# A list scheduler for hand tables in an attention and feed-forward kernel, with softmax normalised per head after the weighing

## Chip, cores and metric

The kernel runs on one core of one Trainium2 chip. The metric is device time in microseconds (us) for one launch. The engines are PE (TensorE, matrix products; PEld is its weight load), DVE (VectorE), ACT (ScalarE), POOL (GpSimd) and SP (SyncE, which issues all DMAs here). Each works through its own queue in order.

## The reference

Two batches, eight heads, 768 positions, 64 features a head. Queries and keys are hashed to 64 buckets by the signs of six projections. The scores of pairs in unequal buckets are masked, a softmax follows, and the result is weighed with v:

```python
mask = q_bucket[:, :, :, None] == k_bucket[:, :, None, :]
scores = np.where(mask, scale * np.matmul(q, k.transpose(0, 1, 3, 2)), -1000000000.0)
attn = np.exp(scores - np.max(scores, axis=-1, keepdims=True))
attn = attn / (np.sum(attn, axis=-1, keepdims=True) + 1e-09)
x = np.matmul(attn, v)        # then (1536 tokens, 512)
h = x @ w_in                  # 512 x 2048
x = (h * (1.0 / (1.0 + np.exp(-h)))) @ w_out
out = ((x @ w1) * (x @ w2) @ w3) @ w_out2   # 512 x 1024, 1024 x 1024, 1024 x 512
```

q, k, v and the projections are float32; the weights are float64.

## The kernel before

Every product is made of three float32r products: an operand is split into a rounded part (h) and the float32r of the rest (l), and h·h, h·l and l·h add up in PSUM. So splitting (a rounding copy, then a subtraction) runs all through the kernel.

**Weights.** A weight comes in pieces of 1024 columns and two steps of 512 columns each (`Piece`, `Step`, lines 125 to 191). A step is one DMA of 512 KB with the float64 words, two scaling copies on ACT (`scale`: the high words as a float, L165, and the low words, L169), two joins on DVE (`join`, L178 and L182; the second puts the sign bit back), and the split on POOL (`split`: L114 rounds, L117 subtracts). Seven pieces and four raw buffers exist.

**Attention.** w3 @ w_out is made ahead, as `wprime`, beside the attention (`combine`, L442: 8 blocks of 24 products), so that the second feed-forward part needs one product less. Two heads form a `Pair` (q and k transposed, a head on each half of the partitions): loads, rounding, rest, projection (L266), bucket bits (L273), then DMAs that gather the operands of each head's scores (L298, L304). A `Unit` is 128 queries of one head, 96 in all:

- `scores` (L342): four products of 384 columns, the mask being part of the operands.
- `peak`, `factor`, `offset` on DVE (L349, L354, L360): the row's negated maximum, 0.125 or 0, and their product. The last has two tensors of one column as inputs.
- `exp` on ACT (L365), with scale and bias from these columns; the instruction also leaves the row's sum.
- `guard` and `invert` on DVE (L372, L376): sum plus 1e-9, and its reciprocal. `norm` on POOL (L379) multiplies the 768 columns of P with it.
- `turn` on PE (L388): six transposes. `split`: ACT rounds (L120, tile `pth`), DVE subtracts (L406, `ptl`).
- `weigh` on PE (L417), for two units at a time: 12 products of 256 columns. `store`: two copies on ACT (L120, `xt` and `X`), one addition on POOL (L431) into X, the tokens' features.

**Order.** It is written by hand. A loop over slots (lines 550 to 590) emits for each slot the steps of up to six units in different stages, then what the tables give for it: `PAIRS` (lines 45 to 55) has the slots of the pairs' jobs, `STEPS` (57 to 79) those of the weights, `FILL` (81 to 86) the number of w3 products, `ON_DVE` what DVE does in POOL's place.

**Feed-forward.** 1536 tokens are three blocks of 512. `Ff1` has 24 cells (8 pieces by 3 blocks) of 48 products, `Ff2` 12 cells of 72: 2016 products of 512 columns. A cell rises (`up_mm`, L194 to L196, then sigmoid on ACT, L655, or a copy, L689, the gate on DVE, L657 or L694, and `split_g`, L602 and L603) and falls (L194 to L196 again, added to X on DVE, L672 or L709). The loop of lines 722 to 729 lets the next cell rise before the last one falls. The steps of the weights still to come are spread over it by `tick` and `advance` (lines 609 to 629). The first rise of a block takes x split by `split_x` (L222, L223). The outputs leave by DMA at L711.

PSUM has eight banks: during the attention four for scores (two tensors of two banks), two for transposes, one for the weighed output, one for w3 products and projections; in the feed-forward eight, four for rises and four for falls.

## Time and profile before

| | |
|---|---|
| median of 3 runs | 782.79 us (782.45 to 785.75) |
| span of the profiled execution | 781.3 us, 11396 instructions |
| busy share: PE, PEld, DVE, ACT, POOL | 96%, 82%, 71%, 55%, 45% |
| queue of SP's DMAs | 26384 packets, 74.14 MB |

The profile is of one execution; its own time is not given apart from its span, from the first to the last instruction. Times of the trace are counted from the span's start. Busy times of PE contain the overlap of pipelined products, so the distance between starts is what a product costs in a row. An idle time in a row is what the engine stood still before it, with the instruction that ended it.

### The profile page before, as it was taken

To read this page: it belongs to the slowest core of one execution; us is meant where nothing else is said; L and a number is where in the kernel's file an instruction comes from. 1 tells how busy PE (TensorE), PEld (TensorE's weight loads), DVE (VectorE), ACT (ScalarE), POOL (GpSimd) and SP (SyncE) were. 2 spreads that over 40 slices of the span, in tenths; PEclk is the share of its full clock that TensorE was granted. 3 is DMA by queue.
4 is the path that set the end of the run, shared out by engine and by line. 5 is a ranking of instruction groups with operands and counts; after the bars stand their busy time and mean duration, and the time that the engine had idled before them with its cause. 6 is when DMAs were issued, how large, how long until landed. Compare 5 with 4: busy or idle time off the path is not lost.

```text
span 781.3 us, 11396 instructions
## 1 busy us (share of the span) xinstructions
PE 746.4 (96%) x3858; PEld 636.9 (82%) x3858; DVE 556.8 (71%) x1153; ACT 429.9 (55%) x848; POOL 348.2 (45%) x364
## 2 busy tenths in 40 slices
PE   6888999899999999999999999999999999999997
PEld 5777888789898888788888888888888888888885
DVE  5999999999999898966777776666685224444233
ACT  4787979799898889775444433432334432221110
POOL 3889888687878677423333322204150102102000
PEclk8689999999999999999999999999999999999999
DMA  8867464646383431322232312203020002000012
GB/s 272 214 178 172 128 154 130 152 143 162 85 207 75 116 122 40 123 81 92 98 101 88 107 58 78 65 16 108 17 90 29 28 27 80 29 0 1 1 54 109
DMA packets 26442, 74.86 MB, mean 96 GB/s; under 512 B 4136, under 2 KB 4136, under 8 KB 26384
## 3 DMA queue, kind: packets, MB, share of 16 engines
q1 hardware_dynamic: 26384, 74.14, 32.8%
q8 instruction: 31, 0.51, 0.3%
q14 instruction: 27, 0.22, 0.1%
HBM read 49.29 MB, written 5.24 MB: 70 GB/s over the span
## 4 chain that ended last, share of the span: by engine, by line
PE 58%; DVE 1%; issue 0%
PE dps L194 6%; PE dps L196 6%; PE dps L195 6%; PE hps L195 5%; PE hps L196 5%; PE hps L194 5%; PE ops L196 3%; PE pb L196 3%; PE pa L196 3%; PE ops L195 3%; PE pb L195 3%; PE pa L195 3%; PE pb L194 3%; PE pa L194 3%; PE ops L194 3%; DVE x L223 1%
## 5 line engine op out<-in xcount | busy, mean ns | idle before, releaser
L379 POOL TENSOR_SCALAR P<-P,st 128x768 f32<-128x768 f32 x96 | 96.5, 1005 | 54.2 <-DVE st L360 46.5
L120 ACT ACTIVATE gh<-g 128x512 fp32r<-128x512 f32 x72 | 45.6, 633 | 114.8 <-DVE g L694 66.2
L365 ACT ACTIVATE P<-sc,st 128x768 f32<-128x768 f32 x96 | 95.0, 989 | 12.7 <-DVE st L360 9.9
L406 DVE TENSOR_TENSOR ptl<-pt,pth 128x384 fp32r<-128x384 f32 x192 | 97.3, 547 | 5.4 <-ACT pth L120 5.1
L603 DVE TENSOR_TENSOR gl<-g,gh 128x512 fp32r<-128x512 f32 x72 | 62.3, 866 | 50.3 <-ACT gh L120 50.3
L349 DVE TENSOR_REDUCE st<-sc 128x1 f32<-128x768 f32 x96 | 91.1, 948 | 9.8 <-PE sc L342 8.0
L120 ACT ACTIVATE pth<-pt 128x384 fp32r<-128x384 f32 x192 | 83.6, 487 | 22.5 <-PE pt L388 21.7
L388 PE MATMUL pt<-ident,P 128*128 128x128 f32 x576 | 82.7, 281 | 11.8 <-POOL P L379 8.0
L114 POOL TENSOR_SCALAR w<-x_w 128x512 fp32r<-128x512 f32 x32 | 20.3, 633 | 158.0 <-DVE x_w L182 137.5
L388 PEld LDWEIGHTS pt<-ident,P 128*128 128x128 f32 x576 | 68.0, 145 | 23.4 <-POOL P L379 17.3
L417 PE MATMUL xo<-pth,V 128*128 128x256 f32 x288 | 81.7, 311 | 4.5 <-ACT X L120 4.2
L694 DVE TENSOR_TENSOR g<-pb,a 128x512 f32<-128x512 f32 x24 | 16.6, 690 | 92.0 <-PE pb L196 92.0
L417 PE MATMUL xo<-ptl,V 128*128 128x256 f32 x288 | 75.5, 290 | 3.5 <-DVE ptl L406 3.4
L195 PE MATMUL dps<-gl,wo 128*128 128x512 f32 x192 | 74.7, 389 | 0.0
L194 PE MATMUL dps<-gh,wo 128*128 128x512 f32 x192 | 74.7, 389 | 0.0
L196 PE MATMUL dps<-gh,wo 128*128 128x512 f32 x192 | 74.7, 389 | 0.0
L655 ACT ACTIVATE sg<-hps 128x512 f32<-128x512 f32 x48 | 28.3, 590 | 80.9 <-PE hps L196 80.9
L417 PEld LDWEIGHTS xo<-pth,V 128*128 128x128 f32 x288 | 55.9, 194 | 11.7 <-ACT X L120 8.9
L417 PEld LDWEIGHTS xo<-ptl,V 128*128 128x128 f32 x288 | 56.3, 195 | 5.3 <-DVE ptl L406 5.0
L442 PE MATMUL wps<-wo,w 128*128 128x512 f32 x192 | 59.0, 409 | 0.0
L342 PE MATMUL sc<-ka,qa 128*128 128x384 f32 x192 | 52.7, 357 | 5.6 <-DMA ka<-khi 3.4
L657 DVE TENSOR_TENSOR g<-hps,sg 128x512 f32<-128x512 f32 x48 | 33.0, 687 | 35.1 <-ACT sg L655 35.1
(187 smaller groups left out, 1913.7 us busy)
## 6 DMA issues: line engine op xcount, KB each, us to landing
raw_w<-in_w SPq DMA_DIRECT2D x32, 512.0 KB
raw_wo<-in_wo SPq DMA_DIRECT2D x24, 512.0 KB
raw_win<-in_win SPq DMA_DIRECT2D x16, 512.0 KB
ka<-khi SPq DMA_DIRECT2D x31, 192.0 KB
qraw<-in_qT SPq DMA_DIRECT2D x8, 384.0 KB
kraw<-in_kT SPq DMA_DIRECT2D x8, 384.0 KB
qa<-qhi SPq DMA_DIRECT2D x16, 192.0 KB
qb<-qhi SPq DMA_DIRECT2D x16, 192.0 KB
```

Source lines behind the costliest of these rows:

```text
L120: nc.scalar.activation(out=dst, in_=src, func=AF.Copy)
L194: nc.tensor.matmul(out=ps, lhsT=whi, rhs=xhi, start=first, stop=False)
L195: nc.tensor.matmul(out=ps, lhsT=whi, rhs=xlo, start=False, stop=False)
L196: nc.tensor.matmul(out=ps, lhsT=wlo, rhs=xhi, start=False, stop=last)
L349: nc.vector.tensor_reduce(out=s[:, 0:1], in_=self.sc[:, :, :HF], op=ALU.max, axis=AX.XY, negate=True)
L365: nc.scalar.activation(out=self.P, in_=self.sc[:, :, :HF], func=AF.Exp, scale=s[:, 1:2], bias=s[:, 2:3], accum_out=s[:, 3:4],)
L379: nc.gpsimd.tensor_scalar(out=self.P, in0=self.P, scalar1=self.st[:, 4:5], scalar2=1.0, op0=ALU.mult, op1=ALU.mult)
L388: nc.tensor.transpose(pt[:, c * 128:c * 128 + 128], self.P[:, g, c * 128:c * 128 + 128], ident)
L406: nc.vector.tensor_tensor(out=l, in0=src, in1=h.bitcast(F32), op=ALU.subtract)
L417: nc.tensor.matmul(out=self.xo[:, :N], lhsT=V[:, c, :], rhs=x[:, c, :], start=(c == 0 and x is self.h), stop=(c == NQ - 1 and x is self.l),)
L442: nc.tensor.matmul(out=ps, lhsT=w[:, a, k], rhs=r[:, b], start=(k == 0 and n == 0), stop=(k == 7 and n == 2))
L603: nc.vector.tensor_tensor(out=l, in0=g, in1=h.bitcast(F32), op=ALU.subtract)
```

## The change

The tables and the slot loop go. Each step of the work becomes an `op` with its engines and their costs in ns, the steps that it depends on, a due time, the buffers that it takes and gives back, and a function that emits it. `Plan.run` then goes through a modelled time: of the engines' ready steps it takes, for each engine, the one that is due first among those that could start within 150 ns of the earliest, and emits the engine's that starts soonest. Steps with more than one engine in their `on` go where the plan puts them. `OFF` moves the due times of each kind of step by a fixed number of us. The due times assume 3 us a unit. w3 products have a `hold` as well, before which the plan does not emit them. In the feed-forward the same plan orders the rises, falls, gates and weight steps of all cells.

Of the computation:

- q is scaled by 0.125 first (`prescale`), and `factor` is then two operations of one tensor each.
- P is not normalised. The row sums of a head gather in `sums`; once a head, DVE adds 1e-9 and inverts (`invert`), PE transposes the inverses (`flip`), ACT unloads them, a DMA stores them to DRAM, a second spreads them over 64 partitions, and POOL multiplies the head's 768 columns of x (`norm`).
- Groups of three units are weighed at once (12 products of 384 columns); the two copies behind go to ACT or DVE (`move`).
- Steps of weights due in the attention get their sign from an activation (`side`) and a product on POOL (`signed`) in place of the second join; scaling the low words may go to POOL; for pieces needed in the first 120 us the split may go to ACT and DVE.
- Feed-forward part one uses tanh of h/2: (tanh + 1) times h, halved as it is added (`more_`).
- Scores, qa, qb, ka and kb have two buffers (the latter had three), raw weights three and one more later (four before). Each PSUM tensor is allocated once for its bank or pair of banks.
- At the hand-over (`hand_over`) the attention's memory is given back and six more PSUM banks join the two for products.

The core of the diff, with the scheduler's choice, the weights, a unit and a head:

```diff
-PAIRS = [
-    dict(zip(JOBS, row))
...
-STEPS = {
...
-FILL = [
...
+SOON, W3_AT, W3_SPAN = 120, 34.7, 23.6
+OFF = {
+    "exp": 1.57, "factor": -0.43, "fall": -3.11, "gate": 5.08, "hi": -5.82, "high": -4.16, "join": -2.5,
+    "lo": -5.04, "low": -1.83, "more_": 8.78, "move": 1.81, "norm": -3.78, "peak": 6.41, "prescale": 1.59,
+    "project": -1.13, "rest": -7.4, "rise": -14.66, "round_": -1.66, "scores": -2.64, "side": -5.88,
+    "sign": 5.02, "signed": -1.18, "split_lo": 5.08, "squash": 6.92, "store": -8.8, "turn": 0.04, "vhi": 3.17,
+    "vlo": -9.35, "weigh": 4.85, "weight": -1.47,
+}
...
+        while todo:
...
+            for e, t in engines.items():
+                could = []
+                for o in wait[e]:
+                    s = max(t, o.ready)
+                    if e == "POOL" or (e == "DVE" and o.port):
+                        s = max(s, port)
+                    for pool, key in o.take:
+                        slots = self.free[pool]
+                        if not slots or (pool in turn and turn[pool][-1] != key):
+                            s = None
+                            break
+                        s = max(s, min(slots, key=lambda x: x[0])[0])
+                    if s is None:
+                        continue
+                    could.append((s, o))
+                if could:
+                    soon = min(s for s, _ in could) + self.PATIENCE
+                    at, pick = min((x for x in could if x[0] <= soon), key=lambda x: (x[1].due, x[0]))
+                    if best is None or at < best[0]:
+                        best = at, e, pick
...
-        def join(self, n, cut=slice(0, STEP)):
...
+                def side(e, raw=raw, x=x):
+                    nc.scalar.activation(out=plan[x], in_=pair(raw)[:, :, 1].bitcast(F32), func=AF.Sign)
+
+                def signed(e, x=x, t=t):
+                    nc.gpsimd.tensor_tensor(out=plan[x], in0=plan[t].bitcast(F32), in1=plan[x], op=ALU.mult)
+                a = op({"ACT": 570}, high, [load], due, [("x", x)])
+                b = op({"ACT": 570, "POOL": 590}, low, [load], due, [("t", t)])
+                j = op({"DVE": 608}, join, [a, b], due + 1, port=True)
+                if need < T_END - 20:
+                    j = op({"ACT": 570}, side, [j], due + 2, give=[raw])
+                    j = op({"POOL": pool2(STEP)}, signed, [j], due + 2.5, give=[t])
+                else:
+                    j = op({"DVE": 608}, sign, [j], due + 2, give=[raw, t], port=True)
...
+            soon = need < BEGIN + SOON
+            h = op({"POOL": pool1(STEP), "ACT": act(STEP)} if soon else {"POOL": pool1(STEP)}, hi, [j, opener], due + 3, take=first)
+            opener = h
+            done.append(op({"POOL": pool2(STEP), "DVE": dve(STEP)} if soon else {"POOL": pool2(STEP)}, lo, [h], due + 4,
...
-            def factor(self):
...
-            def norm(self):
...
+                def factor(e, uk=uk):
+
+                    s = plan[uk("st")]
+                    nc.vector.tensor_scalar(
+                        out=s[:, 1:2], in0=s[:, 0:1], scalar1=BIG / 2, scalar2=1.0, op0=ALU.is_lt, op1=ALU.mult
+                    )
+                    nc.vector.tensor_scalar(
+                        out=s[:, 2:3], in0=s[:, 0:1], scalar1=BIG / 2, scalar2=s[:, 0:1], op0=ALU.is_lt, op1=ALU.mult
+                    )
...
+                sc = op({"PE": 4 * (PE_FREE + HF * PE_COL)}, scores, gathers[par], tu - 3, [("S", uk("S"))])
+                pk = op({"DVE": dve(S)}, peak, [sc], tu - 2.8, [("st", uk("st"))])
+                fa = op({"DVE": 195}, factor, [pk], tu - 2.8)
+                ex = op({"ACT": 985}, exp, [fa, *exps[:1]], tu - 2.7,
+                        [("P", uk("P"))] + ([("sums", hk("sums"))] if i == 0 else []), [uk("S"), uk("st")])
...
+                    tr = op({"PE": 3 * PE_TURN}, turn, [ex, begun, tr if g else None], tu + 0.5, [("T", uk(f"T{g}"))],
+                            give=[uk("P")] if g else [])
+                    opens = g == 0 and i % GRP == 0
+                    a = op({"ACT": act(HF)}, split_hi, [tr, None if opens else opener], tu + 1,
+                           [("pth", gk("pth")), ("ptl", gk("ptl"))] if opens else [])
+                    opener = a if opens else opener
+                    low.append(op({"DVE": dve(HF)}, split_lo, [a], tu + 1.5, give=[uk(f"T{g}")]))
...
+                mv = op({"ACT": 2 * act(N), "DVE": 2 * dve(N)}, move, [xo], tu + 3.5, [("xt", gk("xt"))], [gk("xo")])
+                stores.append(op({"POOL": pool2(N)}, store, [mv], tu + 4, give=[gk("xt")]))
...
+            iv = op({"DVE": 250}, invert, exps, te + 3)
+            fl = op({"PE": 110}, flip, [iv], te + 4, [("W", hk("it"))], [hk("sums")])
+            un = op({"ACT": act(128)}, unload, [fl], te + 4.5, [("wsb", hk("invt"))], [hk("it")])
+            sp = op({"SP": 350}, dma(lambda h=h: inverse[h].rearrange("(i p) -> i p", p=128), lambda hk=hk: plan[hk("invt")][:NQ, :128]),
+                    [un], te + 8, give=[hk("invt")], size=3072)
+            bc = op({"SP": 500}, dma(lambda hk=hk, m=m: plan[hk("invb")][m], lambda h=h: inverse[h:h + 1].to_broadcast([64, S])),
+                    [sp], te + 12, [("invb", hk("invb"))], size=196608)
+            nm = op({"POOL": pool2(S)}, norm, [bc, *stores], te + 20, give=[hk("invb")])
+            last_store[h] = nm
...
+            last = op({"PE": 3 * (PE_FREE + 512 * PE_COL)}, product, [last, *made, *(x for p in wo2p for x in p[1])],
+                      need + k * span / 8 - 2, [("fill", key + ("token",)), ("W", key + ("ps",))] if k == 0 else [],
+                      ([name] + [p[0] for p in wo2p] * (it == DF2 // 128 - 1)) if k == 7 else [],
+                      hold=need + k * span / 8 - 2)
...
+    def hand_over(e):
+        st.close()
+        mp = pool("mp")
+        for bk in (1, 2):
+            xs[bk] = [tiles(mp, f"x{s}{bk}", [128, BLK], F32R, 4) for s in "hl"]
+        plan.buffers("sg", tiles(mp, "sg", [128, BLK], F32, 4))
+        plan.buffers("gh", tiles(mp, "gh", [128, BLK], F32R, 6))
+        plan.buffers("gl", tiles(mp, "gl", [128, BLK], F32R, 6))
+        plan.buffers("raw", tiles(mp, "rawm", [128, 2 * STEP], U32, 1))
+        plan.buffers("fill", [None] * 7)
+        plan.buffers("W", tiles(pool("mps", PSUM), "more", [128, 512], F32, 6))
...
+                def gate(e, key=key, sg=sg):
+                    nc.vector.scalar_tensor_tensor(
+                        out=plan[sg], in0=plan[sg], scalar=1.0, in1=plan[key], op0=ALU.add, op1=ALU.mult
+                    )
+
+                a = op({"ACT": act(BLK)}, squash, [last], d, [("sg", sg)])
+                g = op({"DVE": dve(BLK)}, gate, [a], d + 0.7, give=[key, key + ("token",)])
```

## Rows read from the trace of the kernel before

**Rows 1.** Busy us by stretch: PE, PEld, DVE, ACT, POOL; granted clock, DMA share, GB/s

```profile
0.00:316.00 316.00, 287.59 (x1840) 258.77 (x1841) 291.67 (x775) 264.47 (x565) 238.48 (x254) 0.96 0.55 145
20.00:60.00 40.00, 33.90 (x179) 30.14 (x177) 36.60 (x91) 33.15 (x67) 33.66 (x32) 0.76 0.73 189
60.00:160.00 100.00, 90.47 (x604) 81.19 (x605) 98.51 (x256) 83.97 (x182) 79.87 (x83) 1.00 0.60 154
160.00:316.00 156.00, 150.88 (x1015) 137.18 (x1014) 145.24 (x409) 138.09 (x301) 118.56 (x128) 1.00 0.42 113
326.00:776.00 450.00, 449.95 (x1984) 371.94 (x1983) 254.56 (x368) 158.10 (x271) 102.78 (x105) 1.00 0.17 58
```

**Rows 2.** Instructions in order of time: a gather, the first scores, the feed-forward's first products

```profile
6.31 0.69 SPq L298 DMA_DIRECT2D ka<-khi  x1
...
12.42 0.98 PE L342 MATMUL sc<-ka,qa 128*128 128x384 f32 x2 [3.45 <-DMA ka<-khi]
...
316.42 0.40 PE L194 MATMUL hps<-qhi,win 128*128 128x512 f32 x1
...
319.05 0.50 PE L195 MATMUL hps<-vraw,win 128*128 128x512 f32 x1 [0.73 <-DVE vraw L223]
```

**Rows 3.** The exponential's line by stretch (ACT busy, records, granted clock, DMA share, GB/s)

```profile
20.00:60.00 40.00, 11.45 (x21) 0.76 0.73 189
60.00:160.00 100.00, 33.86 (x64) 1.00 0.60 154
160.00:316.00 156.00, 56.15 (x104) 1.00 0.42 113
```

**Rows 4.** PE in order of time, back to back: start us, us, instruction

```profile
182.49 0.28 PE L417 MATMUL xo<-ptl,V 128*128 128x256 f32 x1
182.61 0.51 PE L342 MATMUL sc<-ka,qa 128*128 128x384 f32 x2
182.96 0.52 PE L342 MATMUL sc<-kb,qb 76*128 76x384 f32 x2
...
186.62 0.82 PE L388 MATMUL pt<-ident,P 128*128 128x128 f32 x6
187.19 0.36 PE L417 MATMUL xo<-pth,V 128*128 128x256 f32 x1
```

**Rows 5.** Groups of instructions on DVE up to 316 us (busy us, mean ns)

```profile
L360 DVE TENSOR_TENSOR st<-st 128x1 f32<-128x1 f32 x96 | 30.3, 316 | 0.0
L182 DVE SCALAR_TENSOR_TENSOR x_w<-raw_w,t_w 128x256 uint32<-128x256 uint32 (+1 forms) x27 | 17.5, 647 | 0.0
...
L376 DVE RECIPROCAL st<-st 128x1 f32<-128x1 f32 x96 | 14.9, 155 | 0.0
...
L372 DVE TENSOR_SCALAR st<-st 128x1 f32<-128x1 f32 x96 | 13.6, 142 | 4.2 <-ACT P L365 4.0
...
L182 DVE SCALAR_TENSOR_TENSOR x_wo<-raw_wo,t_wo 128x512 uint32<-128x512 uint32 x8 | 8.0, 1014 | 0.0
```

**Rows 6.** Single-column operations on DVE: duration ns, least, median, most

```profile
L354 DVE TENSOR_SCALAR st<-st x96: 143/153/157, 15.1 to 308.1; 128x1 f32<-128x1 f32 x96
L360 DVE TENSOR_TENSOR st<-st x96: 140/159/2246, 15.3 to 308.3; 128x1 f32<-128x1 f32 x96
```

**Rows 7.** ACT up to 316 us by groups, and the table load at the sigmoid's line

```profile
L120 ACT ACTIVATE xt<-xo 64x256 f32<-64x256 f32 x47 | 17.8, 379 | 1.1
...
L165 ACT ACTIVATE x_w<-raw_w 128x512 f32<-128x512 f32 x16 | 10.9, 680 | 0.1
...
L655 ACT ACT_TABLE_LOAD  x1: 1283/1283/1283, 321.8 to 321.8; - x1
```

**Rows 8.** Groups of instructions on POOL up to 316 us

```profile
L379 POOL TENSOR_SCALAR P<-P,st 128x768 f32<-128x768 f32 x96 | 96.5, 1005 | 54.2 <-DVE st L360 46.5 <-ACT pth L120 3.1 <-PE xo L417 1.0
L431 POOL TENSOR_TENSOR X<-X,xt 64x256 f32<-64x256 f32 x47 | 36.9, 785 | 7.2 <-ACT X L120 5.1 <-PE wps L442 0.2
...
L117 POOL TENSOR_TENSOR klo<-kraw,khi 128x768 fp32r<-128x768 f32 x7 | 13.1, 1868 | 0.0
```

More of the change, by code (lines that the diff above doesn't have):

```diff
@@ new lines, with dve, dve2, act @@
+PE_FREE, PE_COL, PE_TURN = 13.5, 1 / 2.4, 109.0
+TAIL = {"PE": 220.0, "ACT": 90.0, "DVE": 110.0, "POOL": 150.0, "SP": 40.0, "": 0.0}
+DMA_RATE, DMA_WAIT = 220.0, 2000.0
+def dve(n):
+    return (n + 72) / 0.96
+def dve2(n):
+    return (n / 2 + 72) / 0.96
+def act(n):
+    return 65 + n / 1.2
+def pool1(n):
+    return 80 + n
+def pool2(n):
+    return 130 + 2.2 * n
+class Op:
+    __slots__ = ("on", "emit", "deps", "due", "take", "give", "left", "ready", "end", "heirs", "size", "start", "ran", "port")
+    def __init__(self, on, emit, deps, due, take, give, size):
+        self.on, self.emit, self.due, self.take, self.give = on, emit, due, take, give
+        self.deps = [d for d in deps if d is not None]
+        self.left, self.ready, self.end, self.heirs, self.size = 0, 0.0, None, [], size
@@ new lines, in lsh_attention_moe_kernel, with scaled @@
+    plan.buffers("t", tiles(wp, "t", [128, STEP], U32, 2))
+    plan.buffers("wsb", tiles(wp, "wsb", [128, DM], F32, 1))
+    for nm in ("sg", "gh", "gl"):
+        plan.buffers(nm, [])
+    xs = [[tiles(wp, f"x{s}0", [128, BLK], F32R, 4) for s in "hl"], None, None]
+    def scaled(e, dst, src, by=1.0):
+        if e == "ACT":
+            nc.scalar.activation(out=dst, in_=src, func=AF.Copy, scale=by)
+        elif e == "DVE" and by == 1.0:
+            nc.vector.tensor_copy(out=dst, in_=src)
+        else:
+            engine[e].tensor_scalar(out=dst, in0=src, scalar1=by, scalar2=1.0, op0=ALU.mult, op1=ALU.mult)
@@ L714, in lsh_attention_moe_kernel @@
-    for p in [p for c in range(1, len(p_in)) for p in (p_in[c], p_out[c])] + [
-        p for c in range(len(p_a)) for p in (p_a[c], p_b[c], p_c[c])
-    ]:
-        queue.extend(p.steps())
-    queue[0].load()
-    queue[1].load()
-    work = [Ff1(c, bk) for c in range(len(p_in)) for bk in range(NBLK)]
-    work += [Ff2(c, bk) for c in range(len(p_a)) for bk in range(NBLK)]
-    for a, b in zip([None, *work], [*work, None]):
-        if b:
-            b.rise()
-        if a:
-            a.fall()
-            if a.bk == NBLK - 1:
-                for p in a.pieces:
-                    p.used = True
+                scaled("ACT", pz[half, side, 0, cs], praw[half])
@@ new lines, in lsh_attention_moe_kernel @@
+    NIN, NOUT = DFF // 256, DF2 // 256
+    cells = [(1, c, bk) for c in range(NIN) for bk in range(NBLK)] + [(2, c, bk) for c in range(NOUT) for bk in range(NBLK)]
+    cost = {1: 48 * 0.227, 2: 72 * 0.227}
+    at, t = {}, T_END
+    for cell in cells:
+        at[cell] = t
+        t += cost[cell[0]]
+    uses = {}
+    for cell in cells:
+        uses.setdefault(cell[:2], []).append(cell)
+    pieces = {}
+    for (part, c), of in sorted(uses.items()):
+        need = min(at[x] for x in of)
+        if part == 1:
+            pieces["in", c] = piece(win[c], need)
+            pieces["out", c] = piece(wo1[c], need + 6)
+        else:
+            pieces["a", c] = piece(w1[c], need)
+            pieces["b", c] = piece(w2[c], need + 3)
+            pieces["c", c] = piece(lambda n, c=c: wprime[2 * c + n // DM], need + 8, False, combined[2 * c:2 * c + 2])
@@ new lines, in lsh_attention_moe_kernel, with split_x, high, low @@
+    over = op({"": 0}, hand_over, ended, T_END)
+    def split_x(part, bk, k, deps, due):
+        def high(e):
+            scaled(e, xs[bk][0][k], xraw[:, k, bk * BLK:bk * BLK + BLK])
+        def low(e):
+            sub(e, xs[bk][1][k], xraw[:, k, bk * BLK:bk * BLK + BLK], xs[bk][0][k])
+        a = op({"ACT": act(BLK)}, high, deps, due)
+        return op({"DVE": dve(BLK)}, low, [a], due + 0.5, port=True)
+    ready = {}
+    for bk in range(NBLK):
+        first = min(at[x] for x in cells if x[0] == 1 and x[2] == bk)
+        for k in range(4):
+            heads = [last_store[h] for h in range(2 * H) if h % H // 2 == k and
+                     (bk != 0 or h < H) and (bk != 2 or h >= H)]
+            ready[1, bk, k] = split_x(1, bk, k, heads + ([over] if bk else []), first - 6 + k)
```

1054 lines of the change are left out of this document (498 added, 556 removed).

## The prediction

> **What bounds the kernel now.** I read the busy time stage by stage first, then the pace of the units, then durations and who waits. The windows show two stages that a mean over the span would hide. From 326 to 776 us, the feed-forward products, PE is busy 449.95 of 450 us with 1984 products, 226.8 ns each; DVE has 254.6 us there [rows 1]. Only fewer products could shorten this stage, and the change keeps all 2016. Before it lies the attention, with the products of w3 and w_out beside it, until the first feed-forward product starts at 316.4 us [rows 2]. From 60 to 160 us DVE is busy 98.5 of 100 us and PE 90.5; from 160 to 316 us PE has 150.9 of 156 and DVE 145.2; from 20 to 60 us DVE has 36.6 of 40 and POOL 33.7, and TensorE's granted clock is 0.76, so for part of it the lower of its two levels [rows 1]. The pace says the same. Each of the 96 units (128 queries of a head) leaves two records on the exponential's line: 10.5 units in 40 us (3.81 us a unit), then 32 in 100 us (3.13), then 52 until the attention's end, some 151 us to the last exponential (2.90) [rows 3]. So the bound is the weights' preparation early on, then DVE, then PE. The time is the start of the feed-forward, plus a stretch that PE fixes, plus the tail.
>
> **Part by part.** The sum is made against the profiled span of 781.3 us; the median of the runs is 782.8, 1.5 more, which I add at the end.
>
> *PE.* Back to back, a 256-column product takes 0.12 us, a pair of score products 0.35, six transposes 0.57 [rows 4]. A unit has four score products (0.70), six transposes (0.57) and on average six weighing products (0.72): 2.0 us, 191 for 96 units. The 192 products of w3 and w_out add 43.5 at 226.8 ns, the 96 projections 16.8 at 0.175: 251 us. Groups of three make four 384-column products a unit of six of 256, 0.70 for 0.72, so 2 us go; 16 small transposes of the inverses bring some 1.5 back. PE's sum does not move. With the weights ready its floor is 2.0 + 0.50 (192 products over some 88 units) + 0.175 = 2.68 us a unit, against 2.90 now.
>
> *DVE.* Guard and reciprocal of each unit go, 13.6 + 14.9 = 28.5 us [rows 5]; 16 pairs, one a head, cost 16 x 0.30 = 4.8. The offset's product of two tensors goes, 30.3 us [rows 5], and a second factor with one tensor comes. How long is that? The offset takes 140 ns at least, 159 in the median, 2246 at most; the old factor, as small but with one tensor input, stays within 143 to 157 [rows 6]. So most of the 30.3 is waiting, and I take 0.153, the mean of the nearest row: 14.7 us; the other end is the offset's mean, 0.316. The Trainium skill, SBUF — State Buffer, section Who interferes with whom, says that a DVE instruction with two SBUF inputs contends with a GpSimd instruction that reads SBUF, and one with at most one such input (outside certain fast modes) does not. By it these waits go; without it DVE's sum is 15.6 us higher. The spread of [rows 6] agrees. The second join of 24 weight steps goes to ACT and POOL: 17.5 + 8.0 = 25.5 us [rows 5]. Against that, moves of the weighed output (64 of 384 columns) and rests of early weights (14 steps) may land on DVE: at most 36 and 14, by the nearest rows, the ACT move and the join of the same length [rows 5, 7]. DVE has 291.7 us up to 316 [rows 1]. After: 291.7 - 28.5 + 4.8 - 30.3 + 14.7 - 25.5 = 227, and 277 if both choices fall on it: 2.4 to 2.9 us a unit, around PE's floor.
>
> *ACT.* It has 264.5 us up to 316 [rows 1]. The sign of 24 steps adds 24 x 0.68 = 16, priced by the scaling copy of the same size; the moves, 17.8 for the one shown and as much for its twin, become 64 of half as many columns again, 24 (no longer than now) to 36 (in proportion), or none if DVE takes them; scaling the low words (16) may go to POOL [rows 7]. So 229 to 281 us. That is near the pace too, and the reason why I don't take PE's floor.
>
> *POOL.* It has 238.5 us [rows 1]. The 96 normalisations go (96.5), and 48 additions (36.9) become 32 of half as many columns again (37). In come 16 normalisations of a head (30, at the 1.87 of the other 768-column two-tensor operation), 24 products of 512 columns (30, two thirds of that each) and 8 scalings of q (8, at the 1.0 of the old normalisation) [rows 8]: 210 us, give or take 30 by what the planner hands to ACT and DVE. POOL also waits 46.5 us for DVE's offset ahead of its normalisation [rows 8]; that chain goes, since the exponential feeds the transposes directly. What is late next is the split of the transposes on ACT and DVE.
>
> *SP and the hand-over.* Each head adds a store of its inverses and a load that spreads them, the second waiting for the first, on SP's one queue; behind them stand the gathers and loads of later heads. Those are due 16 us or more ahead of use. A gather whose issue ended at 7.0 let the scores start at 12.4 [rows 2]: 5.4 us a landing, so a head blocks SP for less than that lead, and I price it at nothing. Bare it is only for the last head: sum, inverse, transpose, copy, two landings, normalisation and the split of x, 10 to 15 us after the last exponential. PE covers that with the last weighing, some w3 products and the first cell's 24 rising products (5.4 us), which need the first batch alone. Today x's split makes PE wait here too, 0.73 us in the row shown [rows 2]. I take no difference; the ends are 1 us less and 8 more.
>
> *The rest.* Tanh of half the argument replaces the sigmoid at the same size, the halvings sit in instructions that are there already, and the second table load, 1.28 us at 321.8 [rows 7], lies beside PE's work: nothing. The start, where q is scaled first and ACT and POOL make gathers that DMAs make now: nothing, between 1 less and 2 more. One PSUM tensor a bank and the tail: nothing.
>
> *The sum.* From 20 to 60 us I take 3.3 us a unit, midway between 3.81 and 2.8: POOL and DVE lose work, but transfers and the low clock stay. So about 14.5 units are done at 60 us, in place of 12.5. The other 81.5 at 2.8 us, between the floor of 2.68 and today's 2.90 because four engines lie near each other, take 228: last exponential near 288, feed-forward 6 us later (as now) at 294 instead of 316. 781.3 - 22 = 759.3, and with the 1.5: **761 us**.
>
> **Rivals.**
> - *PE's floor is reached*: 2.9 us a unit early, 2.68 after; 16 units at 60 us, 80 x 2.68 = 214, feed-forward at 280: 747. For it: every other engine can fall below 2.5 a unit. Against: not all at once, and two buffers each for scores, transposes and exponentials.
> - *Only DVE's stretch gains*: PE was already the bound after 160 us, and the early stage is held by transfers and clock. 32 x (3.13 - 2.90) = 7 us: 775. For it: PE's 150.9 of 156. Against: DVE is at 93% there too.
> - *The feed-forward loses its cover* (slower): its order also becomes the planner's. Gate, rounding and rest follow each other on ACT and DVE between rise and fall; where a join or a sum that waits for its data stands ahead of them on DVE's queue, PE waits. Over 36 cells, 0.61 us a cell eats the 22; 1 us a cell gives 797. For it: sums and gates carry fixed offsets of 5 to 9 us in their due times. Against: DVE's 254.6 of 450.
> - *The sign needs another table* (slower; the change would not unload DVE for free, as it says): two loads of 1.283 us [rows 7] for each of 24 steps are 62 us on ACT, some 250 + 62 = 312 before any wait, feed-forward near 336: 802. For it: a load does stand where the sigmoid follows the exponentials. Against: copies and exponentials mix here without one; no row shows the sign. The Trainium skill, ScalarE: Activation LUTs, section Table sets: the hidden batching unit, has cheap functions in every set, without the sign in its list of them; at its 2.66 us a switch the load would be 128 us, an estimate from that page.
> - *Nothing comes of it*: the 7 us of DVE's stretch are eaten by 7 at the hand-over: 782.
>
> **How the numbers follow.** 761 has a chance of 0.50 (752 to 769), PE's floor 0.10, DVE's stretch alone 0.18, no change 0.08, feed-forward gaps 0.11, the table 0.03. A measurement of this kernel tells about 0.5%, 3.9 us. Faster by more: 0.50 + 0.10 + 0.18 = 0.78; within it 0.08; slower 0.14. The range runs from 746, just below the floor case, to 787; outside lie most of the two slower cases.
>
> **What would show it.** Right: the first feed-forward product near 294 us; exponentials 2.8 us apart from 60 us on; DVE below 280 us up to there, its single-column operations all near 0.15; PE full in the feed-forward at 226.8 ns a product; one table load. Wrong: a pace of 2.9 or more with ACT full; PE idle in the feed-forward behind DVE's queue; PE idle for over 6 us at the hand-over for the last head's spread inverses; table loads among the exponentials.

## The result, and the profile after

The changed kernel takes **788.46 us** in the median (787.84 to 789.27, 5 runs) beside 783.92 (5 runs) of the kernel before on the same chip: a ratio of 1.0056, 95% interval 1.0034 to 1.0079. I had said 761, with 787 as the upper end. The profiled run took 789.27 us with a span of 787.6, so 1.7 us lie outside the span. It is the slowest of the five; the profiled run of the kernel before took 782.79, so the two traces lie 6.5 us apart where the medians lie 4.5.

The windows of the changed kernel by stretch, with the columns of [rows 1]:

```profile
0.00:316.00 316.00, 288.63 (x1635) 256.82 (x1636) 281.00 (x615) 260.20 (x543) 200.47 (x187) 0.94 0.63 157
20.00:60.00 40.00, 29.79 (x158) 25.87 (x156) 34.85 (x70) 30.68 (x64) 24.03 (x20) 0.88 0.68 166
60.00:160.00 100.00, 91.55 (x493) 80.08 (x494) 88.98 (x186) 87.03 (x180) 65.64 (x58) 0.90 0.66 166
160.00:316.00 156.00, 153.29 (x935) 138.82 (x934) 144.62 (x336) 132.32 (x284) 102.60 (x95) 1.00 0.57 143
336.00:776.00 440.00, 439.94 (x1941) 363.98 (x1940) 250.07 (x356) 149.52 (x252) 110.49 (x107) 1.00 0.16 54
```

The feed-forward is as full as before (439.94 of 440 us). From 160 us on PE is a little fuller (153.29 of 156 against 150.88). From 20 to 60 us no engine is full: PE has 29.79 of 40 against 33.90 in [rows 1]. Before, DVE was nearly full from 60 to 160 us (98.51); now it is not (88.98).

The exponential's line in the changed kernel, by stretch (ACT busy, records, granted clock, DMA share, GB/s), two records a unit, to be read against [rows 3]:

```profile
20.00:60.00 40.00, 10.11 (x20) 0.88 0.68 166
60.00:100.00 40.00, 9.65 (x18) 0.75 0.61 163
100.00:160.00 60.00, 22.37 (x41) 1.00 0.70 168
160.00:316.00 156.00, 58.69 (x110) 1.00 0.57 143
```

That is 4.0, 4.4, 2.9 and 2.8 us a unit. The kernel before had 3.8 from 20 to 60 us and 3.1 from 60 to 160. So the units are slower up to 100 us and no slower behind it: 21 exponentials start before 100 us, 25 in the kernel before.

PE in order of time around the start of the feed-forward, in the changed kernel:

```profile
317.94 0.27 PE L633 MATMUL acc<-ident,sums 128*6 128x128 f32 x1
319.57 0.44 PE L606 MATMUL acc<-pth,V 128*128 128x384 f32 x1 [1.36 <-ACT wsb L240]
...
323.15 0.39 PE L759 MATMUL more<-xh,piece 128*128 128x512 f32 x1
...
330.88 0.51 PE L759 MATMUL more<-xl,piece 128*128 128x512 f32 x1 [0.73 <-DVE xl L247]
```

The first feed-forward product starts at 323.15 us in place of 316.42 [rows 2]. That is 6.7 us, and the span is longer by 6.3: the whole loss of this run is made before it. From the first to the last feed-forward product it takes 459.9 us, 459.3 before. The wait for the split of x is there as before (0.73).

**Where PE's time goes.** For every two neighbouring products of PE I took the distance of their starts, less the median distance of that kind behind 160 us (174 ns for a weighing product of 384 columns, 120 for one of 256, 175 for a score product, 109 for a transpose, 226.8 for 512 columns). The medians are PE's work; what is over is lost, to waits or to a low clock. The start and the 18 products of the warm-up count as lost. In us, from the profiled run of each kernel:

| | work | 0–20 | 20–60 | 60–100 | 100–160 | 160–336 | last product starts |
|---|---|---|---|---|---|---|---|
| before | 716.5 | 14.0 | 17.3 | 5.3 | 8.2 | 13.2 | 775.7 |
| changed | 714.6 | 13.1 | 17.6 | 16.7 | 5.0 | 14.6 | 783.1 |
| e8, bare weights | 714.8 | 12.6 | 14.6 | 6.5 | 6.7 | 15.1 | 771.3 |
| e11, weights' work as before | 714.6 | 13.0 | 15.3 | 10.6 | 6.3 | 11.4 | 772.3 |
| e16, no normalisation | 714.1 | 12.9 | 14.6 | 12.2 | 3.0 | 11.0 | 768.9 |
| e20, both | 713.9 | 12.8 | 15.1 | 10.3 | 1.6 | 8.0 | 762.9 |

The work fell by 1.9 us and the loss from 60 to 100 us rose by 11.4. Before the change, 36.6 us of a loss of 58 lay in the first 100 us. By the prediction's paces some 29 units were to be started at 100 us in place of 25, so about half of its 22 us was to come from there; behind 100 us there were 21.4 to lose in all.

What the change did to single groups. DVE up to 316 us (busy us, mean ns, idle before):

```profile
L290 DVE SCALAR_TENSOR_TENSOR t<-x,t 128x512 uint32<-128x512 uint32 x30 | 25.5, 871 | 1.6 <-ACT t L280 1.6
L549 DVE TENSOR_SCALAR st<-st 128x1 f32<-128x1 f32 x96 | 19.6, 204 | 0.0
...
L247 DVE TENSOR_TENSOR piece<-x,piece 128x512 fp32r<-128x512 f32 x11 | 10.5, 951 | 0.6 <-ACT piece L240 0.3
...
L242 DVE COPY xt<-acc 64x384 f32<-64x384 f32 x15 | 8.3, 555 | 6.1 <-PE acc L606 5.7
L629 DVE TENSOR_SCALAR sums<-sums 128x6 f32<-128x6 f32 x16 | 6.7, 420 | 0.1
```

The second factor (L549), the join (L290) and the exponential (L555) one by one (ns: least, median, most; first and last start in us):

```profile
L549 DVE TENSOR_SCALAR st<-st x96: 197/204/208, 14.5 to 313.6; 128x1 f32<-128x1 f32 x96
```

```profile
L290 DVE SCALAR_TENSOR_TENSOR t<-x,t x72: 651/683/2345, 24.6 to 666.7; 128x512 uint32<-128x512 uint32 x72
```

```profile
L555 ACT ACTIVATE P<-score,st x96: 967/992/1032, 14.8 to 313.9; 128x768 f32<-128x768 f32 x96
```

ACT, the sign activation up to 316 us and the only table load; then POOL up to 316 us:

```profile
L302 ACT ACTIVATE x<-raw 128x512 f32<-128x512 f32 x24 | 16.2, 674 | 7.2 <-DVE t L290 7.2
...
L240 ACT ACT_TABLE_LOAD x1 | 1.3, 1283 | 0.7 <-PEq L885 0.7
```

```profile
L621 POOL TENSOR_TENSOR X<-X,xt 64x384 f32<-64x384 f32 x30 | 31.3, 1044 | 58.2 <-ACT X L240 33.9 <-DVE X L242 20.8 <-DMA kb<-bits 2.5
L305 POOL TENSOR_TENSOR x<-t,x 128x512 f32<-128x512 f32 x24 | 31.2, 1301 | 22.3 <-ACT x L302 21.9
L640 POOL TENSOR_TENSOR X<-X,invb 64x768 f32<-64x768 f32 x15 | 27.5, 1833 | 5.8 <-DMA invb<-inverse 5.0
```

The terms for ACT and POOL came out near their price. What they do not show is a weight step of which each engine waits for another: DVE's join ends, ACT gives the sign after 7.2 us of waiting in all, POOL stands 21.9 us for it. The waits of SP's queue and of PE in two stretches (us in total, times, longest), the first from 20 to 130 us, the second from 30 to 80:

```profile
SPq L269 <- ACT x L302: 39.8, 12, 7.5
SPq L376 <- ACT wsb L240: 11.3, 3, 4.7
```

```profile
PE turn L573 <- DVE ptl L247: 7.3, 6, 2.1
PE score L533 <- ACT P L555: 3.9, 2, 1.9
PE acc L606 <- DVE ptl L247: 2.5, 2, 1.8
```

SP stands 39.8 us ahead of raw loads (L269), for the sign activation that gives their buffer back; in the kernel before it was 15.6, for the join. The first w3 product starts at 90.7 us, 73.8 before.

### The profile page after: what moved, and what is told of

Read it like the earlier page. It is cut to its first block, busy times and chain, and to the rows that moved or that the text cites. A ratio compares the mean times of both kernels' runs of the same rounds, so it can differ in the third digit from the quotient of the medians.

```text
span 787.6 us, 10761 instructions
## 1 busy us (share of the span) xinstructions
PE 753.0 (96%) x3682; PEld 639.7 (81%) x3682; DVE 545.5 (69%) x989; ACT 420.9 (53%) x816; POOL 320.2 (41%) x301
## 4 chain that ended last, share of the span: by engine, by line
PE 77%; DVE 15%; ACT 3%; DMA 2%; issue 1%; POOL 0%; ACTq 0%; DVEq 0%; POOLq 0%; SPq 0%
PE more L810 21%; PE more L759 18%; PE acc L759 13%; PE acc L606 6%; PE turn L573 5%; PE score L533 5%; DVE ptl L247 4%; PE acc L810 4%; DVE st L539 3%; PE acc L669 3%; PE acc L422 2%; DVE t L290 1%; DVE xl L247 1%; ACT pth L240 1%; ACT P L555 1%
## 5 line engine op out<-in xcount | busy, mean ns | idle before, releaser
L759 PE MATMUL more<-xh,piece 128*128 128x512 f32 x464 | 163.7, 389 | 0.0
L810 PE MATMUL more<-gh,piece 128*128 128x512 f32 x308 | 113.0, 389 | 0.0
L247 DVE TENSOR_TENSOR ptl<-turn,pth 128x384 fp32r<-128x384 f32 x192 | 98.3, 548 | 11.4 <-ACT pth L240 10.9
L759 PE MATMUL acc<-xh,piece 128*128 128x512 f32 x304 | 104.6, 389 | 0.0
L759 PEld LDWEIGHTS more<-xh,piece 128*128 128x128 f32 x464 | 87.1, 188 | 18.0
L573 PE MATMUL turn<-ident,P 128*128 128x128 f32 x576 | 88.9, 288 | 13.3 <-DVE ptl L247 12.6
L555 ACT ACTIVATE P<-score,st 128x768 f32<-128x768 f32 x96 | 95.1, 990 | 11.2 <-DVE st L549 9.6
L240 ACT ACTIVATE pth<-turn 128x384 fp32r<-128x384 f32 x192 | 85.8, 488 | 22.5 <-PE turn L573 21.4
L539 DVE TENSOR_REDUCE st<-score 128x1 f32<-128x768 f32 x96 | 90.8, 946 | 5.2 <-PE score L533 4.8
L759 PE MATMUL more<-xl,piece 128*128 128x512 f32 x232 | 90.8, 391 | 1.7 <-DVE xl L247 1.6
L290 DVE SCALAR_TENSOR_TENSOR t<-x,t 128x512 uint32<-128x512 uint32 x72 | 56.1, 790 | 10.8 <-ACT x L276 9.1
```

Source lines behind the costliest of these rows:

```text
L240: nc.scalar.activation(out=dst, in_=src, func=AF.Copy, scale=by)
L247: engine[e].tensor_tensor(out=dst, in0=src, in1=hi.bitcast(F32), op=ALU.subtract)
L290: engine[e].scalar_tensor_tensor(out=plan[t], in0=plan[x].bitcast(U32), scalar=3, in1=plan[t], op0=ALU.logical_shift_left, op1=ALU.bitwise_or,
L539: nc.vector.tensor_reduce(out=plan[uk("st")][:, 0:1], in_=plan[uk("S")][:, :, :HF], op=ALU.max, axis=AX.XY, negate=True)
L555: nc.scalar.activation(out=plan[uk("P")], in_=plan[uk("S")][:, :, :HF], func=AF.Exp, scale=s[:, 1:2], bias=s[:, 2:3], accum_out=plan[hk("s ...
L573: nc.tensor.transpose(pt[:, c * 128:c * 128 + 128], P[:, g, c * 128:c * 128 + 128], ident)
```

## The experiments

**First: the clock, DVE's order, POOL.** The granted clock is 0.82 from 20 to 100 us, 0.88 before; DVE's subtraction of the transposes stands in PE's waits; rests of early weights run on DVE.

```diff
+                    for g in range(2 if u < 28 else 0):
+                        nc.tensor.matmul(out=sc[:, g, :HF], lhsT=plan[hk("qa")][:, qs],
+                                         rhs=plan[hk("ka")][:, g * HF:g * HF + HF], start=True, stop=True)
```

> The changed kernel with the first two score products of units 0 to 27 written twice (the second time over the first), so PE has 0.35 us more per unit at full clock; the order of every queue is unchanged. Theory 1, the lower clock: between 20 and 100 us the granted clock (0.82 there) lets PE's steps take double their planned time, the queues' order no longer fits, and 5 units are lost. Then with more PE work the clock stays near 1.0 from 30 us on, more than 24 units are exponentiated by 100 us instead of 21 to 22, and the feed-forward starts 6 to 12 us before 323 us: 777 to 783. Theory 2, DVE's queue order, and theory 3, DVE's two-input operations blocked by POOL: PE only gets more to do, the pace stays and the time is 787 to 795, even if the clock rises.

788.25 us (784.59 to 789.88), 1.0047 (1.0024 to 1.007). In its profiled run, the fastest, the clock was 0.94 from 20 to 100 us and the first feed-forward product came at 318.6. In that run PE's loss before 100 us is 35.1 us in place of 47.4 and its work 9.8 us more. In the median the added work and the better clock cancel; the clock is not the cause by itself.

```diff
...
-"split_lo": 5.08
+"split_lo": -3.0
...
```

> The changed kernel with the due time of the transposes' rest (split_lo) moved from 5.08 us late to 3 us early, so that DVE takes it ahead of weight joins, rests and moves. Theory 2, DVE's queue order: PE's waits for that rest (12.6 us before transposes on PE, 25.7 on the weight loads) fall by at least half, and the feed-forward starts 6 to 12 us earlier than 323 us: 777 to 783. Theory 1, the clock, and theory 3, the port: the waits change place, the weights and with them the w3 products come later, and the time is 786 to 794.

792.67 us, 1.0102 (1.0069 to 1.0135). The 21st unit came 8.7 us earlier, the first w3 product 4.3 later, at 95.0. PE's waits for the rest of the transposes fell from 12.6 to 6.4 us up to 330 us, as theory 2 said, but those of the scores for an exponential rose from 5.7 to 19.5.

```diff
-            ns = o.on[e]
+            ns = o.on[e] * (2 if e == "PE" and at < 90000 else 1)
```

> The changed kernel, planned with PE's costs doubled up to 90 us of planned time; the work is the same, only the order changes. Theory 1, that the order does not fit a PE at its lower clock: with an order made for a slow PE the queues stop waiting for the wrong thing, 2 to 4 more units are done by 100 us and the time is 776 to 784. Theory 2 and theory 3: nothing about DVE's share is mended, the time is 786 to 795.

792.98 us, 1.011 (1.0081 to 1.014): a plan that reckons with a slow PE early on does not help.

```diff
-SOON, W3_AT, W3_SPAN = 120, 34.7, 23.6
+SOON, W3_AT, W3_SPAN = 0, 34.7, 23.6
```

> The changed kernel with the rounding and the rests of the early weight pieces on POOL alone, as before the change (in it 11 rests take 10.5 us on DVE, 9 of them between 20 and 100 us, and 10 roundings are on ACT). Theory 2, DVE's queue: DVE has 9 us less between 20 and 100 us, PE waits less for the rests of the transposes, the feed-forward starts 3 to 8 us earlier: 780 to 785. Theory 3, the port: POOL has more two-input work, the joins on DVE (1105 ns each between 20 and 100 us, 0.68 alone) get longer, above 1.2 us, and nothing is won: 787 to 795. Theory 1: within 3 us of 788.

790.33 us, 1.0077 (1.0047 to 1.0106). The units kept the pace of before up to 60 us (12 started from 20 to 60); then the bucket bits came late. POOL weighed them at 91.5 us, behind a weight step's product, rounding and rest, SP issued their gather at 94.7, and it landed 8.8 us later. PE stood for it, as this line of its PE in order of time shows:

```profile
103.64 0.66 PE L533 MATMUL score<-kb,qb 76*128 76x384 f32 x1 [5.97 <-DMA kb<-bits]
```

None of the three held. Theory 1 misses in e1 and e3, theory 2 in e2 and e4. Theory 3 has every time right, but its sign did not come: in e4 the joins from 20 to 100 us took 1009 ns in the mean in place of 1105, not above 1200. In e2 and e4 the relief moved the loss to another wait.

**Second: the weights' work.** Theory 4 was that the longer chain of a weight step, and SP's queue behind it, cost the first 100 us.

```diff
-GRP = 3
+GRP = 2
```

> Units are weighed in groups of two, as before the change, everything else as changed. Two hundred and fifty-six columns a weighing product in place of 384: by the paces of the two kernels (120 and 174 ns a product, 576 and 384 of them) PE has 2.3 us more to do, moves and additions come 48 times in place of 32. Theory 4 (the loss of the first 100 us is the longer chain of each weight step, with the raw words held until its sign is read, and SP's queue behind it): no help, 788 to 793 us, first feed-forward product 323 to 327. Rival (groups of three make PE and the transposes' buffers wait for the third unit early on): 781 to 786, more than 20 exponentials started in 20 to 60 us less than 2 apart is not needed, but at least 3 units more by 100 us.

789.55 us, 1.0062 (1.0044 to 1.008), as theory 4 had it: the groups are not shown to cost anything.

```diff
-                if need < T_END - 20:
+                if False:
```

> The sign comes back by a second join on DVE in every step, as before the change (no sign activation, no product on POOL), everything else as changed. ACT loses 24 x 0.6, POOL 24 x 1.26, DVE gains 24 x 0.7 to 1.1 us = 17 to 26 us. Theory 4 (longer weight chain): the raw words come free two engines earlier, SP's wait for them falls from 40 to below 20 us up to 130 us, the first w3 product starts before 85 us instead of 90.7, first feed-forward product 314 to 319, 779 to 784 us. Rival 5 (DVE is what the first 100 us hang on, by its place in the chain of waits): the added joins go in at their length, first feed-forward product 324 to 332, 789 to 797 us.

791.68 us, 1.0099 (1.0075 to 1.0123). SP's wait for raw buffers fell to 18.9 us as theory 4 said, but the time did not follow: against theory 4 in its form for this place alone. It is no clean test of SP's queue, because SP's waits for the tile of the inverses and of wprime rose from 11.3 to 21.2 us.

```diff
...
-                a = op({"ACT": 570}, high, [load], due, [("x", x)])
+                a = op({"ACT": 570}, high, [load], due, [("x", x)], [raw] if early else [])
...
-                j = op({"DVE": 608}, join, [a, b], due + 1, port=True)
+                j = a if early else op({"DVE": 608}, join, [a, b], due + 1, port=True)
...
```

> Of the 24 weight steps due in the attention only the load, one copy of the high words and the split are left; the low words, the join, the sign activation and the product on POOL are left out (wprime is made of other numbers). It asks what the attention does by itself under the new order. Theory 4 (weights): most of PE's lost time between 20 and 100 us (34 us over the products' own paces, 22 before the change) goes: first feed-forward product 298 to 308, 763 to 773 us. Rival 6 (the order, two score buffers and two transpose banks hold the units back whatever the weights do): 20 units or fewer started in 20 to 100 us, first feed-forward product 314 to 323, 779 to 788 us.

777.2 us, 0.9904 (0.9876 to 0.9931), the first feed-forward product at 312.4. Between the two theories: left out, this part of the weights' work gives 11 us. A loss of 33.7 us before 100 us stays, with only the load, one copy and the split of each step left.

```diff
-SOON, W3_AT, W3_SPAN = 120, 34.7, 23.6
+SOON, W3_AT, W3_SPAN = 0, 34.7, 23.6
...
-                if need < T_END - 20:
+                if False:
...
-                mv = op({"ACT": 2 * act(N), "DVE": 2 * dve(N)}, move, [xo], ...
+                mv = op({"ACT": 2 * act(N)}, move, [xo], ...
```

> The weights' chain as before the change: both joins on DVE, roundings and rests of all pieces on POOL, and the moves of the weighed output on ACT alone; the planner, the normalisation once a head, the groups of three and the rest as changed. Theory 4 (the weights' new chain costs the first 100 us): pace of the early units at least as before the change (23 or more started in 20 to 100 us), first feed-forward product 308 to 316, 773 to 781 us. Rival 6 (the order and its few buffers): 20 or fewer in that stretch, first feed-forward product 320 to 328, 785 to 793 us. Rival 5 (DVE's load): DVE gains 17 to 26 us of joins and loses 9 x 1.0 of rests and up to 36 of moves, so 318 to 324, 783 to 789 us.

**777.72 us, 0.993 (0.9908 to 0.9952)**: faster than both kernels. With the work back that the change handed between ACT, POOL and DVE, the kernel is 10.8 us faster. Its windows, with the columns of [rows 1], have 66.4 us of PE from 20 to 100 us where the changed kernel has 62.7:

```profile
20.00:60.00 40.00, 32.15 (x173) 27.73 (x172) 35.84 (x77) 31.92 (x69) 24.99 (x23) 0.88 0.78 180
60.00:100.00 40.00, 34.21 (x185) 30.60 (x184) 33.89 (x71) 31.73 (x66) 31.15 (x27) 0.90 0.64 184
```

Four more runs fill the table of the three places (sign, rests, moves):

> Only the two copies of the weighed output are held on ACT, as before the change (in the changed kernel DVE makes some 36 of the 64 up to the feed-forward, about 0.56 us each, 20 us); signs and rests as changed. Theory A (each of the three places adds its own amount: sign on DVE alone +3.2, rests on POOL alone +1.9, all three -10.8, so the moves alone -15.9): 771 to 776 us. Theory B (they help only together: the sign product leaves POOL so that POOL can take the rests, and the joins and rests that DVE exchanges are as many): 786 to 791 us.

> Sign by a second join on DVE and early roundings and rests on POOL alone, moves where the plan puts them. Theory A (amounts add): 788.5 + 3.2 + 1.9 = 793.6, so 791 to 796 us. Theory B (sign and rests change places between DVE and POOL and help only together): 776 to 782 us, first feed-forward product 312 to 318, more than 21 units started in 20 to 100 us.

> Early roundings and rests on POOL alone and moves on ACT, sign by activation and product as changed. Theory A: 788.5 + 1.9 - 15.9 = 774.5, so 772 to 777 us. Theory B: POOL keeps 24 products of 1.26 us and takes the rests too, so the bucket bits that it weights come late as in the run with the rests alone: 786 to 792 us.

> Sign by a second join on DVE and moves on ACT, early roundings and rests where the plan puts them. Theory A: 788.5 + 3.2 - 15.9 = 775.8, so 773 to 779 us. Theory B: DVE has the second joins and the rests too in the first 100 us: 787 to 792 us.

| put back | median us | put back | median us |
|---|---|---|---|
| none | 788.46 | sign, rests (e9) | 787.11 |
| sign (e6) | 791.68 | rests, moves (e12) | 787.13 |
| rests (e4) | 790.33 | sign, moves (e13) | 785.35 |
| moves (e7) | 789.48 | all three (e11) | 777.72 |

Theory A (amounts add) falls. Theory B holds for e7, and for e12 in its time; e9 and e13 miss its numbers, by 5 and 2 us. Each place put back alone costs 1 to 3 us, each pair gains 1 to 3, all three gain 10.8. Only the last is beyond what another order of the same steps does (e18, below), and the kernel before itself had medians from 783.57 to 785.74 us in the sets of runs that are compared here. That one place put back loads an engine that still has the work of the others would explain the table, but is not shown. Counted as in the table of PE's losses, e13 loses 38.7 us before 100 us, as little as e11 (38.9; the changed kernel 47.4), but from 100 to 336 us 24.6 where e11 loses 17.7. So part of what separates these kernels arises late, where e18 alone makes 24.0 of the changed kernel's 19.6.

**Third: the normalisation, SP's queue, the clock once more, the order.**

```diff
-            sp = op({"SP": 350}, dma(lambda h=h: inverse[h]...
+            sp = op({"ACT": 60}, lambda e, h=h, hk=hk: nc.scalar.dma_start(out=inverse[h]...
...
-        combined.append(op({"SP": 400}, dma(lambda it=it: wprime[it]...
+        combined.append(op({"ACT": 60}, lambda e, it=it, key=key: nc.scalar.dma_start(out=wprime[it]...
```

> The kernel with the weights' work as before (e11, 777.7 us), and the stores of the inverses and of wprime issued by ACT, which makes their tile, in place of SP. SP then no longer stands still for that tile (20.9 us between 20 and 130 us in e11's trace). Theory C (SP's one queue holds gathers and loads up behind such waits, and the units with them): first feed-forward product 306 to 311, 769 to 774 us. Rival D (gathers come early enough; what limits the early units is the path exponential, transposes, split on ACT and DVE): 775 to 780 us.

> The same on the changed kernel (788.5 us), where SP waits 11 us for that tile and 40 for the raw buffers between 20 and 130 us. Theory C: 783 to 786 us, the raw wait stays. Rival D: 787 to 791 us.

787.96 us, 1.0037 (1.0016 to 1.0059), and 789.8 us, 1.0056 (1.0031 to 1.0082). SP no longer waits for that tile, and e11 loses its gain (10.2 us by the medians, 8.4 by the ratios to the kernel before in the same set of runs); the changed kernel, with the same ratio as without it, loses nothing. Theory C is not borne out; e15 is in the range of rival D, e14 misses both. What e14 loses, it loses late: up to 100 us 25 units start and PE loses 38.5 us, as in e11 (25 and 38.9), and from 100 to 336 us it loses 26.8 in place of 17.7. From 160 to 320 us PE's transposes wait 6.1 us for DVE's rests of earlier ones, 0.3 us in e11.

```diff
-            iv = op({"DVE": 250}, invert, exps, te + 3)
...
-            nm = op({"POOL": pool2(S)}, norm, [bc, *stores], te + 20, give=[hk("invb")])
+            nm = op({"": 0}, lambda e: None, [*stores, *exps], te, give=[hk("sums")])
```

> The changed kernel without the normalisation: the guard, the inverse, its transpose, its copy, both DMAs and the product on POOL are left out for all 16 heads (x stays unnormalised). By the prediction's terms they are 5 us of DVE, 1.5 of PE, 30 of POOL, and nothing on SP. Theory C (its DMAs hold up SP's queue, the prediction priced them wrongly): first feed-forward product 312 to 317, 777 to 782 us. Rival D: its own 1.5 us of PE and 3 of the wait for the last head, so 784 to 788 us.

775.53 us, 0.9881 (0.9848 to 0.9915): 12.9 us, where I had priced some 4.5. It is more than either theory said. PE's own work falls by 0.5 us, and from the start of the last exponential to the feed-forward it takes 9.3 us (9.2 with the normalisation), so the rest is pace: 24 units start before 100 us in place of 21.

> The kernel with the weights' work as before (e11), and the first two score products of units 0 to 27 written twice, the first time into the same banks (56 more products, 9 us of PE at the upper clock level, some of it in idle time). In e11 the granted clock is 0.92, 0.88 and 0.90 in 0 to 20, 20 to 60 and 60 to 100 us, which is 10 us of running time lost at most. Theory E (the low clock of the early stretch sets the pace there): clock near 1.0 from 20 us on and 770 to 776 us in spite of the added products. Rival D: 778 to 786 us.

781.47 us, 0.9959 (0.9934 to 0.9984), with a clock of 0.96 from 20 to 100 us in place of 0.89: slower than e11 by 3.8. Theory E falls for this kernel; the added products cost more than the better clock gives back.

```diff
-    PATIENCE = 150.0
+    PATIENCE = 130.0
```

> The changed kernel with the planner's window of 150 ns made 130: no step, cost or buffer changes, only which of nearly equal steps is emitted first. Theory F (differences of some us between these kernels are accidents of the order): away from 788.5 by 3 to 8 us either way. Theory G (the order as such is worth little, the steps decide): 787 to 790 us.

> The weights' work as before (e11) and the normalisation left out as in e16. If the two are separate losses they add: 788.5 - 10.8 - 12.9 = 764.8, so 762 to 768 us, first feed-forward product 300 to 304. If they are one loss, which either relieves: 772 to 778 us, 309 to 314.

e18: 792.57 us, 1.0127 (1.0093 to 1.0161), 4.1 us away by another order of the same steps, 5.6 by the ratios. So a difference of that size between two of these kernels says nothing of its cause. e20: **768.16 us**, 0.981 (0.9771 to 0.9848): 20.3 us below the changed kernel, where 23.7 were the sum, at the upper end of what separate losses were to give. In the time the two are separate losses for the most part. By stretch they are not: before 100 us PE loses 38.9 us in e11, 39.7 in e16 and 38.2 in e20, of 47.4, and behind it, up to 336 us, 17.7, 14.0 and 9.6, of 19.6. In the first 100 us either gives nearly what both give, and what adds up lies later. Its windows show it for PE (columns as in [rows 1]):

```profile
20.00:60.00 40.00, 32.57 (x171) 27.71 (x170) 34.63 (x73) 32.18 (x65) 23.21 (x23) 0.88 0.72 182
60.00:100.00 40.00, 34.09 (x186) 31.37 (x186) 32.92 (x69) 33.04 (x67) 24.20 (x23) 0.90 0.62 167
100.00:160.00 60.00, 60.00 (x371) 55.46 (x370) 55.78 (x125) 55.65 (x118) 41.78 (x42) 1.00 0.75 186
```

From 100 to 160 us PE is full; from 20 to 100 it has 66.7 of 80.

## Why the prediction was wrong

**The step that failed** is the pace of the early units: "From 20 to 60 us I take 3.3 us a unit", then 2.8 from 60 us on. Measured were 4.0 us a unit from 20 to 60 us and 4.4 from 60 to 100. By the prediction 28.8 units are started at 100 us (14.5 and 40 / 2.8); it was 21, and 7.8 units at 2.8 us are 22 us. Behind 100 us, 75 units took 213.9 us, 2.85 each: 4 us more than said. From the start of the last exponential to the feed-forward it took 9.2 us in place of 6, 3 us more (6.9 before; the 5.9 "as now" count from the exponential's end, 8.2 in the changed kernel). Together 29, which is 323.2 - 294. POOL and DVE did lose work from 20 to 60 us, as the prediction's reason has it (24.0 us for 33.7, 34.9 for 36.6), and the pace fell all the same. I had spread the engines' sums evenly over the attention, but 12 joins and 9 of the rests on DVE fall in 20 to 100 us, where the kernel before, too, lost most of its time. A lower sum on an engine says little there, since none is full: the waits listed above are for DVE in one place and for ACT in the next. Of PE's loss of 47.4 us before 100 us the weights' work as before takes 8.5 away (e11), the normalisation left out 7.7 (e16), both 9.2 (e20), which brings it near the 36.6 of the kernel before. Which single wait carries this is not shown.

**The normalisation once a head** was priced by its instructions, and at nothing on SP. Left out, it gives 12.9 us, and 9.6 on top of e11. That is beyond e18's 4.1, so it costs something like 10 us; by which of its parts was not settled. Its stores on SP's queue are not shown to be it: SP's waits for the tile of the inverses and of wprime are 11.3 us from 20 to 130 us, and 12.4 in the kernel before, for wprime alone. One direct cost is in the rows: PE waits 1.36 us until ACT has emptied the accumulator bank that the transposed inverses held (at 319.57 us, above).

**The weights' work** was priced by DVE's sum. DVE's sum did fall, from 291.7 to 281.0 us up to 316, yet above my range. With the moves (16.6 us) and rests (10.5) that the plan put there, my terms give 254. One reason is that I subtracted rows from a busy time, and DVE's rows overlap; these are from the kernel before, in order of time:

```profile
182.15 0.15 DVE L372 TENSOR_SCALAR st<-st 128x1 f32<-128x1 f32 x1 [0.38 <-ACT P L365]
182.22 0.14 DVE L354 TENSOR_SCALAR st<-st 128x1 f32<-128x1 f32 x1
182.34 0.16 DVE L376 RECIPROCAL st<-st 128x1 f32<-128x1 f32 x1
```

Up to 316 us the durations add up to 340 us before and to 314 in the changed kernel: they fell by 26 us, the busy time by 10.7. The other reason is prices: the second factor took 204 ns where I took 153 (4.9 us in all), the sum and inverse of a head 9.8 us for 16 where I took 4.8. This kernel with all of the weights' work put back, and 273 us on DVE up to 316, is 10.8 us faster. The same step has three more pairs, and its size hangs on the rest of the kernel: by the ratios it gives 9.9 us here, 5.6 without the normalisation (e16 to e20), 6.9 with the added products (e1 to e17) and 1.5 with the stores on ACT (e15 to e14). The direction is shown four times, the size is not.

**What held.** PE's work: I said it would not move, it fell by 1.9 us. PE's floor of 2.68 a unit was right (257.6 us of work up to the feed-forward, in 96 units, without the warm-up), but over the attention the pace does not reach it. In part that was luck: at 109 ns each, six transposes take 0.65 us and not 0.57, and the w3 products spread over 96 units are 0.45 and not 0.50. 2.8 behind 100 us was a good choice. The feed-forward kept its cover. POOL has 200.5 us (I said 210), ACT 260.2 (229 to 281). The rival with a table for the sign is false: one load in the whole trace, at 0.7 us, none behind the 24 sign activations. The Trainium skill, SBUF — State Buffer, section Who interferes with whom, has a DVE instruction with two SBUF inputs contend with a GpSimd instruction that reads SBUF. The trace agrees: the factor with one tensor now stays within 197 to 208 ns where the old product ran up to 2246 [rows 6], and the join, with two, takes from 651 to 2345. What the longer joins cost in time no run shows.

**Still open:** the 38 us that even e11 and e20 lose before 100 us. 13 of them lie in the first 20 us, as in every kernel of the table. Bare weights leave 33.7 (e8), a better clock 30.9 with 9.8 us more work (e17), SP's stores on ACT 38.5 (e14).

## What to carry over

Split PE's time into its work and what is lost, by stretch, before pricing a change: a sum that falls on another engine is worth at most what PE loses in the stretches where that engine is the late one. Busy time is a union of rows that may overlap, so add up durations and busy time separately before subtracting one from the other. Where no engine is full, work handed from one to another can add waits, and parts of it put back one by one may show nothing of what all of them together are worth. With a planner's order, measure first what another order of the same steps does, read smaller differences as nothing, and repeat a larger one in a second kernel.

## What was not expected of the hardware

A DVE instruction on one column whose second scalar is a column too takes 204 ns, with an immediate there 154 (L549 and L546, 96 times each); the next instruction starts 122 and 71 ns after them in the median. The store of 16 small tiles and of wprime from ACT's queue in place of SP's, which removes a wait of 20.9 us on SP, made e11 10 us slower and the changed kernel no slower; why was not found.
